# Projecting a tile's heads while its attention still runs: readiness queues, priorities and moved loads in a statically scheduled attention kernel

## The chip, the cores and the metric

The kernel runs on one core of one Trainium2 chip. The metric is the device time of one execution in microseconds (us). Each run's times are compared with runs of the kernel before on the same chip.

## The reference

Two independent attention blocks, A and B, of the same shape are computed and their outputs are put side by side. Cut to what matters:

```python
# per block: x [8, 144, 640], k_cache and v_cache [8, 32, 512, 128], wq [640, 4096], wo [4096, 640], bf16
q = (x @ wq).reshape(8, 144, 32, 128).transpose(0, 2, 1, 3)
scores = einsum("bhqd,bhkd->bhqk", q, k_cache) * 128 ** -0.5
p = softmax(scores)
o = einsum("bhqk,bhkd->bhqd", p, v_cache)
y = o.transpose(0, 2, 1, 3).reshape(8, 144, 4096) @ wo
# result: concatenate([y_A, y_B], axis=-1)
```

## The kernel before

The kernel records operations, each with an engine, an estimated duration and the buffers that it reads and writes. A list scheduler then fixes the order of each engine, in windows of 24 operations, and emits the instructions with the semaphore waits that the buffers ask for. So PE (matmuls), ACT (activations and evictions), DVE (vector work) and the load queue (SP) each run a fixed order, and an operation that waits holds up everything behind it on its engine.

A "tile" is one batch element of one block: 16 tiles, numbered 0 to 15, of four groups of eight heads. In a group PE projects Q (into ps_q, moved to qt_sb by ACT), multiplies with K (ps_s), DVE takes the maximum, ACT the exponential, DVE normalises, PE transposes (ps_pt), DVE copies, PE multiplies with V (ps_o), ACT evicts to otm_sb (the 128 main query rows) and otr_sb (the remaining 16 rows). The output projection takes otm_sb per tile, and otr_sb once per block for all eight batch elements ("the remainder"). Each projection is 32 matmuls of 512 columns and 32 of 128.

```python
# the output projection: "fillers", put between the operations of the NEXT tile's attention
for k in range(H // 4):
    res.append(mk_a(k))          # four heads, 512 columns, PSUM bank ps_out
res.append(ev_a)                 # ACT evicts
for k in range(H // 8):
    res.append(mk_b(k))          # eight heads, 128 columns, same bank
res.append(ev_b)
res.append(dma_out)
...
before(0, lambda: load_wq(0, 0))
before(0, lambda: load_xT(0, 0))
for g in range(1, NG):
    before(g, lambda g=g: load_wq(0, g))
if XH == 2:
    before(1, lambda: load_xT(0, 1))
for hg in range(NHG):
    before(min(2 + hg // 2, NG - 1), lambda hg=hg: load_wo(0, hg))
...
for blk in range(2):
    for b in range(NB):
        fill_state[1] = max(1, FILL_SLOTS // (len(fillers) + 1)) if fillers else 1
        for g in range(NG):
            attention_group(blk, b, g, gi, fillers)   # pops a filler now and then
            ...
        while fillers:
            fillers.pop(0)()
        ...
        fillers.extend(outproj_ops(blk, b))
        if b == NB - 1:
            fillers.extend(outproj_ops(blk, NB))      # the remainder
            ...
while fillers:
    fillers.pop(0)()             # tile 15 and the last remainder stand at the very end
```

Of the kernel before, what the change touches and what calls it, by code (L numbers as in the profile page):

```python
# [22 lines left out]
NPT_BANKS = 2  # L23
SCHED_WINDOW = 24
MODEL_ONLY = False
_DBG = {}


# [23 lines left out]
class _Sched:  # L52
# [3 lines left out]
        self.readers = {}  # L56

    def add(self, eng, fn, reads=(), writes=(), dur=100.0, dma=None, name="", prio=None):
        op = _Op(len(self.ops), eng, fn, tuple(reads), tuple(writes), float(dur), dma, name,
                 len(self.ops) if prio is None else prio)  # L60
        for r in op.reads:
            for w in self.writers.get(r, ()):
                op.preds[w] = "raw"
        for r in op.writes:
            for rd in self.readers.get(r, ()):
                if rd != op.idx and rd not in op.preds:
                    op.preds[rd] = "war"
            for w in self.writers.get(r, ()):
                if w not in op.preds:
                    op.preds[w] = "waw"  # L70
        for r in op.reads:
            self.readers.setdefault(r, []).append(op.idx)
        for r in op.writes:
            if self.readers.get(r) or r not in self.writers:
                self.writers[r] = [op.idx]
            else:
                self.writers[r].append(op.idx)
            self.readers[r] = []
            if r in op.reads:
                self.readers[r] = []  # L80
        self.ops.append(op)
        return op
# [73 lines left out]
def _mm_ns(n):  # L156
    return max(29.0, 2.6 + n * 0.4167)


def _dve_ns(n, mode=1, ptr=0):  # L160
    return 64.0 + n / (0.96 * mode) + 60.0 * ptr


def _act_ns(n, ptr=0, acc=False):
    return 63.0 + n / 1.2 + 88.0 * ptr + (90.0 if acc else 0.0)


def bass_concat_heads__gqa_block_cached__mha_block_cached__near_ridge_kernel(
# [17 lines left out]
    NB, SQ, D = A_x.shape  # L186
    _, H, SK, DH = A_k_cache.shape
# [10 lines left out]
    NG = H // 8  # L198
# [17 lines left out]
    with ExitStack() as st:  # L216
# [62 lines left out]
        def load_wq(blk, hg):  # L279
            wq = blks[blk][3]  # L280
            src = wq.rearrange("(c p) n -> p c n", p=128)[:, :, hg * 1024:(hg + 1) * 1024]
            dst = wq_sb[:, :, hg * 1024:(hg + 1) * 1024]

            def f(e):
                return e.dma_start(dst, src)
            S.add("sp", f, writes=[("wq", hg)], dur=200, dma=(("wq", hg), 128 * NCH * 1024 * 2, "pl"),
                  name="wq%d.%d" % (blk, hg))
# [68 lines left out]
        def softmax_rn(tiles, tag):  # L356
            t0 = tiles[0][0]
            n = len(tiles)
            assert all(tiles[i][0] == t0 + i for i in range(n))

            def f_r(v):
                return v.reciprocal(rr_sb[:, t0:t0 + n], rs_sb[:, t0:t0 + n])  # L362
            S.add("dve", f_r, reads=[("rs", t0 + i) for i in range(n)],
                  writes=[("rr", t0 + i) for i in range(n)], dur=61 + 2 * n, name="R" + tag)
            for i, (ts, pslot) in enumerate(tiles):
                def f_n(v, ts=ts, pslot=pslot):
                    return v.tensor_scalar(p_sb[:, pslot, :], p_sb[:, pslot, :], rr_sb[:, ts:ts + 1], None, ALU.mult)  # L367
                S.add("dve", f_n, reads=[("rr", ts), ("P", pslot)], writes=[("P", pslot)],
                      dur=_dve_ns(512, 4, 1), name="N%s.%d" % (tag, i))

        def attention_group(blk, b, g, gi, fillers):
            gs = gi % NQG
            bs = b % NOB
            slots = load_kv(blk, b, g)
            half = b // BPH
            tg = "%d.%d.%d" % (blk, b, g)

            def fill():
                fill_state[0] += 1
                if fillers and fill_state[0] % fill_state[1] == 0:  # L380
                    fillers.pop(0)()

            for pi in range(4):
                e = 0 if pi < 2 else 1
# [81 lines left out]
            for pi in range(4):  # L466
# [70 lines left out]
                def f_oe(a, pi=pi):  # L537
# [4 lines left out]
                S.add("act", f_oe, reads=[("PSO",)],  # L542
                      writes=[("OTm", bs, g, pi), ("OTr", blk, b, g, pi)],
                      dur=_act_ns(256) + _act_ns(32), name="Oe%s.%d" % (tg, pi))
                fill()

        ost_ctr = [0]

        def outproj_ops(blk, b):
            rem = (b == NB)  # L550
            os_ = ost_ctr[0] % NOS
            ost_ctr[0] += 1
# [4 lines left out]
            def lhs(h):  # L557
                return otr_sb[:, blk, h, :] if rem else otm_sb[:, bs, h, :]
# [7 lines left out]
            def mk_a(k):  # L566
                def go():
                    def f(t):
                        ins = None
                        for h in range(4 * k, 4 * k + 4):  # L570
                            ins = t.matmul(ps_out[:, 0:512], lhs(h), wo_sb[:, h, 0:512],  # L571
                                           start=(h == 0), stop=(h == H - 1))
                        return ins
                    reads = [("wo", (4 * k) // 8)]
                    for h in range(4 * k, 4 * k + 4, 2):
                        reads += rd(h)
                    S.add("pe", f, reads=reads, writes=[("PSOUT",)], dur=4 * _mm_ns(512),
                          name="OPa%s.%d" % (tg, k))
                return go

            def mk_b(k):
                def go():
                    def f(t):
                        ins = None
                        for h in range(8 * k, 8 * k + 8):
                            ins = t.matmul(ps_out[:, 0:D2], lhs(h), wo_sb[:, h, 512:D],  # L586
                                           start=(h == 0), stop=(h == H - 1))
                        return ins
                    reads = [("wo", k)]
                    for h in range(8 * k, 8 * k + 8, 2):  # L590
                        reads += rd(h)
                    S.add("pe", f, reads=reads, writes=[("PSOUT",)], dur=8 * _mm_ns(D2),
                          name="OPb%s.%d" % (tg, k))
                return go

            def ev_a():
                def f(a):
                    return a.copy(ost_sb[:, os_, 0:512], ps_out[:, 0:512])  # L598
                S.add("act", f, reads=[("PSOUT",)], writes=[("ost", os_, 0)], dur=_act_ns(512),
                      name="OEa" + tg)  # L600

            def ev_b():
                def f(a):
                    return a.copy(ost_sb[:, os_, 512:D], ps_out[:, 0:D2])
                S.add("act", f, reads=[("PSOUT",)], writes=[("ost", os_, 1)], dur=_act_ns(D2),
                      name="OEb" + tg)

            def dma_out():
# [12 lines left out]
                              writes=[("out", blk, "r", bb)], dur=200,  # L621
                              dma=(("outr", bb), 16 * D * 2, "pl"), name="OD%s.%d" % (tg, bb))

            for k in range(H // 4):
                res.append(mk_a(k))
            res.append(ev_a)
            for k in range(H // 8):
                res.append(mk_b(k))
            res.append(ev_b)
            res.append(dma_out)  # L630
            return res

        setup_ops()
        FILL_SLOTS = 18 * NG
        fill_state = [0, 1]
        pre = {}

        def before(gi_, fn):
            pre.setdefault(gi_, []).append(fn)

        before(0, lambda: load_wq(0, 0))
        before(0, lambda: load_xT(0, 0))
        for g in range(1, NG):
            before(g, lambda g=g: load_wq(0, g))
        if XH == 2:
            before(1, lambda: load_xT(0, 1))
        for hg in range(NHG):
            before(min(2 + hg // 2, NG - 1), lambda hg=hg: load_wo(0, hg))

        gi = 0  # L650
        fillers = []
        for blk in range(2):
            for b in range(NB):
                fill_state[0] = 0
                fill_state[1] = max(1, FILL_SLOTS // (len(fillers) + 1)) if fillers else 1
                for g in range(NG):
                    for fn in pre.get(gi, ()):
                        fn()
                    attention_group(blk, b, g, gi, fillers)
                    gi += 1  # L660
                    if blk == 0 and b == NB - 1:
                        load_wq(1, g)
                while fillers:
                    fillers.pop(0)()
                if blk == 0 and XH == 2 and b == BPH - 1:
                    load_xT(1, 0)
                if blk == 0 and b == NB - 1:
                    load_xT(1, XH - 1)
                fillers.extend(outproj_ops(blk, b))
                if b == NB - 1:  # L670
                    fillers.extend(outproj_ops(blk, NB))
                    if blk == 0:
                        for hg in range(NHG):
                            fillers.append(lambda hg=hg: load_wo(1, hg))
        while fillers:
            fillers.pop(0)()

        engines = ("pe", "act", "dve", "pool", "sp")
        order = S.schedule(engines, window=SCHED_WINDOW)
# [99 lines left out]
```

## Time and profile before

| | kernel before |
|---|---|
| time, median of the first 5 runs | 809.24 us |
| profiled span | 809.1 us |
| PE, DVE, ACT busy | 92%, 90%, 76% |
| tile 0 ends | 93.0 us |
| a steady tile (4 to 6) | 46.0 us |
| from the last eviction to the end | 19.3 us |

The end of a tile is read from the timeline: 16 small casts to otr_sb belong to each tile, and the end of the 16th is the tile's end. PE's busy time contains the pipeline of its matmuls (a 512-column one lasts 381 ns in the mean, but they follow each other every 216), so 92% is not 92% of what PE can do; the prediction therefore counts matmuls times their spacing. Its fences show the busy shares, the stretches, the load queue and the chain at the end.

### The profile page before, as it was taken

What the parts mean: (1) busy time and instruction counts of PE and PEld (TensorE: products, weight loads), DVE (VectorE), ACT (ScalarE), POOL (GpSimd) and SP (SyncE); (2) the same over time, 40 slices, a digit from 0 to 9 for tenths busy, and PEclk for the clock granted to TensorE, in tenths of its full rate; (3) what the DMA queues carried; (4) which work ended last, traced back from release to release, by engine and by line L of the source; (5) the groups of instructions that cost most, each with busy time, mean ns of one, the idle gap of its engine ahead of it and who ended that gap; (6) DMA issues with size and microseconds to landing.
All of it is one profiled execution on the core that took longest, in us unless ns stands there. A gap on an engine that the chain in (4) does not pass through costs nothing.

```text
span 809.1 us, 23020 instructions
## 1 busy us (share of the span) xinstructions
PE 747.8 (92%) x8946; PEld 569.2 (70%) x9088; DVE 724.6 (90%) x1858; ACT 615.8 (76%) x1957; POOL 0.7 (0%) x6
## 2 busy tenths in 40 slices
PE   3768999999999999999999989999999999999996
PEld 2545687777777777777777667777777778777763
DVE  3665999999999999999998879999999999999990
ACT  2555788888888788888876768788888888888861
POOL 0000000000000000000000000000000000000000
PEclk9789999999999999999999999999999999999999
DMA  9999999989899988799999999997798878888600
GB/s 208 270 275 283 232 247 210 196 182 182 174 227 206 201 182 195 180 213 249 246 218 245 316 234 219 205 194 184 172 201 192 191 179 189 185 187 189 158 5 17
DMA packets 362476, 162.59 MB, mean 201 GB/s; under 512 B 281216, under 2 KB 357248, under 8 KB 362368
## 3 DMA queue, kind: packets, MB, share of 16 engines
q1 hardware_dynamic: 362368, 161.12, 89.6%
q8 instruction: 72, 1.18, 0.7%
q14 instruction: 36, 0.29, 0.1%
HBM read 88.08 MB, written 2.95 MB: 113 GB/s over the span
## 4 chain that ended last, share of the span: by engine, by line
PE 64%; DVE 20%; ACT 8%; DMA 4%; issue 2%; SPq 1%; ACTq 0%
PE ps_q L392 14%; PE ps_o L527 13%; PE ps_out L571 12%; PE ps_pt L500 10%; DVE nm_sb L346 9%; PE ps_s L479 7%; ACT p_sb L350 5%; DVE ptg_sb L516 4%; DVE p_sb L367 4%; PE ps_s L421 4%; PE ps_out L586 2%; ACT otm_sb L540 2%; PE ps_pt L446 2%; DMA kt_sb<-in_B_k_cache_dram 2%; DVE ptg_sb L461 1%
## 5 line engine op out<-in xcount | busy, mean ns | idle before, releaser
L350 ACT ACTIVATE p_sb<-ps_s,nm_sb 128x512 bf16<-128x512 f32 x576 | 396.3, 695 | 49.0 <-DVE nm_sb L346 26.9
L346 DVE TENSOR_REDUCE nm_sb<-ps_s 128x1 f32<-128x512 f32 x576 | 382.3, 680 | 37.7 <-PE ps_s L479 25.2
L392 PE MATMUL ps_q<-xT_sb,wq_sb 128*128 128x144 bf16 x2560 | 207.2, 230 | 16.1 <-DMA xT_sb<-in_A_x_dram 12.3
L392 PEld LDWEIGHTS ps_q<-xT_sb,wq_sb 128*128 128x128 bf16 x2560 | 175.0, 99 | 44.7 <-issue 17.5
L516 DVE COPY ptg_sb<-ps_pt 128x1024 bf16<-128x1024 bf16 x256 | 174.2, 685 | 13.8 <-PE ps_pt L500 12.7
L367 DVE TENSOR_SCALAR p_sb<-p_sb,rr_sb 128x512 bf16<-128x512 bf16 x576 | 181.9, 346 | 2.3
L527 PE MATMUL ps_o<-ptg_sb,v_sb 128*128 128x144 bf16 x2048 | 172.1, 228 | 7.1 <-DVE ptg_sb L516 4.6
L527 PEld LDWEIGHTS ps_o<-ptg_sb,v_sb 128*128 128x128 bf16 x2048 | 136.8, 98 | 43.0 <-DVE ptg_sb L516 21.0
L500 PE MATMUL ps_pt<-id_sb,p_sb 128*128 128x128 bf16 x2048 | 157.0, 221 | 5.5 <-DVE p_sb L367 4.5
L479 PE MATMUL ps_s<-kt_sb,qt_sb 128*128 128x512 bf16 x392 | 145.9, 387 | 15.5 <-ACT p_sb L350 10.6
L540 ACT CAST otm_sb<-ps_o 128x256 bf16<-128x256 f32 x256 | 94.8, 370 | 72.2 <-PE ps_o L527 67.5
L500 PEld LDWEIGHTS ps_pt<-id_sb,p_sb 128*128 128x128 bf16 x2048 | 131.2, 114 | 22.4 <-DVE p_sb L367 14.0
L403 ACT ACTIVATE qt_sb<-ps_q 128x288 bf16<-128x288 f32 x256 | 106.1, 414 | 48.6 <-PE ps_q L392 46.2
L571 PE MATMUL ps_out<-wo_sb,otm_sb 128*128 128x512 bf16 x493 | 128.1, 381 | 3.4 <-DMA wo_sb<-in_B_wo_dram 1.0
L350 ACT ACTIVATION_READ_ACCUMULATOR p_sb<-ps_s,nm_sb 128x1 f32 x576 | 119.6, 208 | 0.0
L571 PEld LDWEIGHTS ps_out<-wo_sb,otm_sb 128*128 128x128 bf16 x512 | 48.7, 98 | 45.6 <-DMA wo_sb<-in_B_wo_dram 1.2
L479 PEld LDWEIGHTS ps_s<-kt_sb,qt_sb 128*128 128x128 bf16 x512 | 48.0, 98 | 43.8 <-ACT p_sb L350 21.1
L362 DVE RECIPROCAL rr_sb<-rs_sb 128x2 f32<-128x2 f32 (+1 forms) x320 | 49.5, 156 | 5.1 <-ACT p_sb L350 4.7
L541 ACT CAST otr_sb<-ps_o 128x32 bf16<-128x32 f32 x256 | 50.0, 195 | 0.0
L421 PE MATMUL ps_s<-kt_sb,qt_sb 128*32 128x512 bf16 x512 | 40.2, 392 | 3.5 <-DMA kt_sb<-in_B_k_cache_dram 2.1
L586 PE MATMUL ps_out<-wo_sb,otm_sb 128*128 128x128 bf16 x512 | 38.6, 219 | 1.7 <-issue 1.0
L586 PEld LDWEIGHTS ps_out<-wo_sb,otm_sb 128*128 128x128 bf16 x512 | 32.2, 98 | 4.2 <-ACT ost_sb L598 1.2
(19 smaller groups left out, 135.2 us busy)
## 6 DMA issues: line engine op xcount, KB each, us to landing
v_sb<-in_A_v_cache_dram SPq DMA_DIRECT2D x64, 512.0 KB, 4.3
v_sb<-in_B_v_cache_dram SPq DMA_DIRECT2D x64, 512.0 KB, 4.3
wq_sb<-in_A_wq_dram SPq DMA_DIRECT2D x4, 1280.0 KB, 7.2
wo_sb<-in_A_wo_dram SPq DMA_DIRECT2D x4, 1280.0 KB, 12.9
wq_sb<-in_B_wq_dram SPq DMA_DIRECT2D x4, 1280.0 KB, 7.5
wo_sb<-in_B_wo_dram SPq DMA_DIRECT2D x4, 1280.0 KB, 8.7
out_dram<-ost_sb SPq DMA_DIRECT2D x16, 160.0 KB, 3.7
kt_sb<-in_A_k_cache_dram SPq DMA_TRANSPOSE x64, 5.8
```

Of the source, the lines that this page charges most:

```text
L346: return v.tensor_reduce(nm_sb[:, ts:ts + 1], ps_s[:, sbank, :], AXL.X, ALU.max, negate=True)
L350: return a.activation(p_sb[:, pslot, :], ps_s[:, sbank, :], ACTF.Exp, bias=nm_sb[:, ts:ts + 1], scale=1.0, accum_out=rs_sb[:, ts:ts + 1])
L367: return v.tensor_scalar(p_sb[:, pslot, :], p_sb[:, pslot, :], rr_sb[:, ts:ts + 1], None, ALU.mult)
L392: ins = t.matmul(ps_q[:, uu * SQ:(uu + 1) * SQ], wq_sb[:, c, h * 128:(h + 1) * 128], xT_sb[:, c, b * SQ:(b + 1) * SQ], start=(c == 0), sto ...
L403: return a.mul(qt_sb[:, gs, 2 * pi:2 * pi + 2, off:off + SQ], ps_q[:, 0:2 * SQ].rearrange("p (u q) -> p u q", u=2), SCALE,)
L479: return t.matmul(ps_s[:, sbank, :], qt_sb[:, gs, u, qoff:qoff + 128], kt_sb[:, slot, (u % 4) * SK:(u % 4 + 1) * SK], start=True, stop=True,)
L500: ins = t.transpose(ps_pt[:, kpt, (uu * 4 + c) * 128:(uu * 4 + c + 1) * 128], pv[:, c, :], id_sb[:],)
L516: return v.tensor_copy(dst, src)
L527: ins = t.matmul(ps_o[:, uu * SQ:(uu + 1) * SQ], v_sb[:, slot, u % 4, c * 128:(c + 1) * 128], ptg_sb[:, gs, u, c, :], start=(c == 0), stop ...
L540: a.copy(otm_sb[:, bs, h0:h0 + 2, :], src[:, :, 0:128])
L571: ins = t.matmul(ps_out[:, 0:512], lhs(h), wo_sb[:, h, 0:512], start=(h == 0), stop=(h == H - 1))
L586: ins = t.matmul(ps_out[:, 0:D2], lhs(h), wo_sb[:, h, 512:D], start=(h == 0), stop=(h == H - 1))
```

## The change

Its intent: do not keep the projection of a tile for the next tile, but put each piece into a queue and let it go once the heads it reads are recorded as done; so that only little stands behind the last tile. Four things change together: the queues with a closer filling stride (a piece may be let go at every second filling point between the attention's operations); a priority table in the scheduler (the projection 150 places later, the Q projection and its eviction 40 earlier) with slightly other duration estimates; the order of the loads; and a second PSUM bank (ps_q, free by then) with its own queue for the last remainder.

```diff
+PRIO = {"OPa": 150, "OPb": 150, "Qp": -40, "Qe": -40}
+FILL_STRIDE = 2
...
-                 len(self.ops) if prio is None else prio)
+                 len(self.ops) + PRIO.get(kind, 0))
...
 def _dve_ns(n, mode=1, ptr=0):
-    return 64.0 + n / (0.96 * mode) + 60.0 * ptr
+    return 65.0 + n / (0.96 * mode) + 64.0 * ptr
...
+                heads_done[(blk, b)] = 8 * g + 2 * pi + 2
...
-            for k in range(H // 4):
-                res.append(mk_a(k))
-            res.append(ev_a)
+            for k in range(H // OPA_HEADS):
+                res.append((OPA_HEADS * (k + 1), (OPA_HEADS * k) // 8, mk_a(k)))
+            res.append((H, None, ev_a))
...
+        before(0, lambda: load_xT(0, 0))
         before(0, lambda: load_wq(0, 0))
-        before(0, lambda: load_xT(0, 0))
...
-            before(1, lambda: load_xT(0, 1))
+            before(BPH * NG - NG, lambda: load_xT(0, 1))
...
-            before(min(2 + hg // 2, NG - 1), lambda hg=hg: load_wo(0, hg))
+            before(NG + hg if NB > 1 else NG - 1, lambda hg=hg: do_load_wo(0, hg))
...
+        def eligible(item):
+            blk, b, nh, hg, fn, tsn = item
+            if hg is not None and (blk, hg) not in wo_loaded:
+                return False
+            if b == NB:
+                return all(heads_done.get((blk, bb), 0) >= nh for bb in range(NB))
+            return heads_done.get((blk, b), 0) >= nh
...
+                tile_ops = outproj_ops(blk, b)
+                queues[0].extend(tile_ops)
...
+                    if last and g == NG - 1:
+                        queues[1].extend(outproj_ops(blk, NB, acc=ps_q, acc_res=("PSQ",)))
```

## The prediction

> **What bounds the kernel now.** I read the page's busy shares first, then the windows view cut at tile ends, then the timeline of start and end. A "tile" is one batch element of one block: four groups of eight heads, 16 tiles in all. Its end is the 16th small cast at L541 that belongs to it, counted in the timeline. Those ends are 92.9, 136.4, 181.9, 227.5, 273.7, 319.3, 365.5, 411.1, 465.6, 515.7, 561.2, 606.8, 653.1, 698.8, 744.9 and 789.7 us; so most tiles take 45.4 to 46.2 us, and four stretches stand out: tile 0 (92.9), tile 8 (54.5), tile 9 (50.1) and 19.4 us after the last tile.
>
> ```profile
> PE 747.8 (92%) x8946; PEld 569.2 (70%) x9088; DVE 724.6 (90%) x1858; ACT 615.8 (76%) x1957; POOL 0.7 (0%) x6
> ...
> DMA  9999999989899988799999999997798878888600
> ```
>
> ```profile
> 12.00:93.00 81.00, 62.73 (x612) 43.52 (x618) 52.19 (x130) 45.78 (x138) 0.00 (x0) 0.87 1.09 266
> ...
> 182.00:228.00 46.00, 44.97 (x558) 34.93 (x565) 45.02 (x116) 38.37 (x123) 0.00 (x0) 1.00 0.93 182
> ...
> 411.00:466.00 55.00, 52.58 (x611) 39.12 (x618) 45.32 (x115) 39.86 (x127) 0.00 (x0) 1.00 1.07 258
> 466.00:516.00 50.00, 47.26 (x581) 37.04 (x592) 45.98 (x122) 38.13 (x124) 0.00 (x0) 0.97 1.04 224
> ...
> 790.00:809.00 19.00, 11.61 (x99) 6.82 (x98) 0.00 (x0) 1.70 (x4) 0.00 (x0) 0.93 0.06 18
> ```
>
> Columns: stretch, length, busy us of PE, PEld, DVE, ACT, POOL, then clock, DMA share, GB/s. In an ordinary tile (182 to 228) PE and DVE are both busy 98%: nothing idle is left to fill. In tile 0 DVE works 52 of 81 us while DMA moves 266 GB/s against 182 later: the start is **bound by loads**. In 411 to 466, where tile 7 and the remainder rows of block A are both projected, DVE has slack: that tile is **bound by PE**. After 790 only PE works.
>
> Why the start is slow stands in the timeline of the load queue:
>
> ```profile
> 28.99 4.07 SPq L326 DMA_TRANSPOSE kt_sb<-in_A_k_cache_dram  x1
> 33.10 0.58 SPq L331 DMA_DIRECT2D v_sb<-in_A_v_cache_dram  x1
> 33.73 0.52 SPq L285 DMA_DIRECT2D wq_sb<-in_A_wq_dram  x1
> 34.28 2.93 SPq L295 DMA_DIRECT2D wo_sb<-in_A_wo_dram  x2
> 37.33 12.43 SPq L326 DMA_TRANSPOSE kt_sb<-in_A_k_cache_dram  x1
> ```
>
> The K transpose behind three weight loads occupies the queue 12.43 us instead of about 3.9. From 33.73 to 49.76 the queue handled three weight loads and one K: 16.0 less 3.9 is 12.1 us, **4.0 us per weight load**. The next group repeats it (55.02 to 70.85: 11.9 us for three).
>
> The tail is the last part of the chain of work that ended last:
>
> ```profile
> 789.79 1.05 PE ps_out L571 x4
> ...
> 791.51 1.98 PE ps_out L586 x32
> ...
> 794.05 6.87 PE ps_out L571 x31
> ...
> 801.59 1.98 PE ps_out L586 x32
> ```
>
> These are the last four wide matmuls of tile 15, its 32 narrow ones, then all 64 of the remainder, serialised by evictions in one bank (ps_out). From PE's end at 803.56 to 809.1 there are 5.5 us of eviction and store.
>
> **What the Trainium skill says.** "TensorE: Matmul & The Clock Gate", section Back-to-back issue gap, puts the isolated warm gap at N/2.4 + 2.5 ns: 215.8 for 512 columns, 62.5 for 144, 55.8 for 128. The trace agrees: 31 matmuls of 512 in 6.85 us, last one 0.38 long, is 216 ns; 32 of 128 in 1.96 us is 56 ns. I use these gaps, not the rows' means (381 and 219 ns), which contain the pipeline. "Perfetto Trace Analysis", section Optimization Strategy, says that where the most-contended engine changes over time, interleaving those regimes may help. That is the intent here: tail and start are the other regimes. "DMA: Bandwidth & Descriptors", section Issuing engines are not separate DMA queues, says all DMAs run on the same 16 engines; the 12.43 us issue agrees that weights and K share one capacity. So moving weights later relieves tile 0 but charges tile 1.
>
> **The change, part by part.** Counts are of the built program: matmuls on PE between tile ends, times the gaps above (a packed 32-column matmul at a quarter of 216). No arithmetic is added: 711.9 us of PE work before, 711.5 after, DVE work the same. How time relates to that work is read from before: tiles with 42.8, 43.0, 43.8 us of PE work took 45.4, 45.6, 46.2, and the double tile with 52.3 took 54.5. So a tile takes its **PE work plus about 2.3 us**, if loads arrive and DVE's 45 us allow.
>
> *Loads.* wo moves from groups 2 and 3 to groups 4 to 7, one per group; the second half of x moves to group 12. Tile 0 then has one weight load per group. Going on from the first V pair issued at 17.2, each group costs 4.0 for wq and 2 x 4.5 for its K and V, 13.0 in all: the last K of tile 0 leaves the queue at 55.6 instead of 75.4, about 20 us sooner. But tile 1 now has the wo loads, again 13.0 per group against some 11.4 of compute: its last K leaves at 55.6 + 52 = 107.6, against 112.5 before. Before, tile 0 ended 17.5 us after its last K, 4.3 us of it out-projection that is now gone; I take 15 for tile 1: **122.6 instead of 136.4**, 14 us gained. (xT now precedes wq at the very start; I give that 0 to 1.5 us.)
>
> *Backlog.* Tile 0 has no wo, so its projection moves on: the order puts 0 us of projection in tile 0, 6.8 in tile 1, 14.8 in tile 2, 9.5 in tile 3 (before: 4.3, 7.9, 8.5, 8.7). Tiles 2 and 3 hold 46.8 and 46.9 us of PE work, so about 49 each against 45.4 and 45.6: **7 us given back**. Tiles 4 to 7 hold 43.1, 43.4, 43.3, 45.0, a sum of 174.8 plus 9.2, or 184.0 against 183.6 measured: nothing.
>
> *Block change.* Tile 7's projection is nearly complete when tile 7 ends, so tile 8 holds 45.6 us of PE work instead of 52.3: 47.9. Tile 9 gets 47.4 instead of 44.0. The four wo loads of block B still go out together behind the remainder's projection; before, tile 9 took 50.1 where its 44.0 plus 2.3 gives 46.3, so I charge some 3 us for them again: 52.7. Together 100.6 against 104.6: **4 us gained**.
>
> *Steady tiles 10 to 14.* Work shifts by tenths; 0. Tile 15 holds 42.9 against 41.4: 1 us lost.
>
> *Tail.* After the last value product the order has 12 wide and 64 narrow matmuls: 12 x 0.216 + 64 x 0.056 = 6.2 us, with ps_q as a second bank hiding the evictions. Plus 0.3 and the 5.5 us of last eviction and store: 12.0. Before it was 19.4: **7.4 us gained**.
>
> Sum: -14 + 7 + 0.4 - 4 + 1 - 7.4 = -17. 809.2 - 17 = 792; finer placing of projections and earlier Q projections (priority -40) may take a little from the waits, so I put 791.
>
> **Rivals.**
> 1. *PE is not the bound in steady tiles, DVE is* (724.6 us less 4.6 of memsets, over 16 tiles, is 45.0 of some 45.7). Then the backlog in tiles 2 and 3 fits partly into slack, and only some 3 us return: about 785. For it: DVE's 98%. Against: the 2.3 us rule also fits the double tile, in which DVE had slack.
> 2. *The load bill is only postponed.* Bytes up to tile 1's end fall only by half of x, so the load gain could shrink to the 5 us by which the last K leaves sooner: about 800. For it: DMA share 1.09. Against: before, by the end of tile 1, K ran nearly two groups ahead, a lead which the change can spend.
> 3. *The fixed order hits new waits*: held ps_out accumulations, or Q projections placed ahead of weights not yet landed, which block PE in order. Some 5 to 10 us in the start or at the block change: 797 to 801. For it: the chain before shows a 7.80 us wait for wq in tile 0; against: wq now comes sooner.
>
> **Range and chances.** 2% faster is 793.1, near my sum; loads are the uncertain term (5 to 18 us), then the steady tiles (12 of them, each 0.5 us either way: 6 us). So 780 to 802, and 0.57 for faster, 0.41 for the same, 0.02 for slower, which would take two of the rivals at their worst.
>
> **What would show it.** Tile 0 should end near 71, tile 1 near 123, tiles 2 and 3 take about 49 each, tiles 4 to 7 184 together, tiles 8 and 9 about 101 together, and the end come 12 us after the last cast. The weight loads should no longer stretch a K issue past about 8 us in the first 60 us. If tile 1 ends after 128, rival 2 holds; if tiles 2 and 3 take 46, rival 1; if steady tiles change by over 0.5 us, the priorities do more than I allow, and my sum is wrong there.

## The result

The changed kernel takes **792.42 us** in the median of 9 runs (790.32 to 796.33) against 809.24 us (15 runs, 806.55 to 813.28). The ratio is 0.9795, with a 95% interval of 0.9773 to 0.9816. So it is about 2% faster; whether by more or less than 2% is not decided by the interval. Ratios here and below are the mean time of one kernel's fast runs over that of the other's of the same rounds, so not quite the ratio of the medians.

The page of the changed kernel, in the lines that answer to those shown of before:

```profile
PE 737.7 (93%) x8939; PEld 567.1 (72%) x9088; DVE 719.9 (91%) x1858; ACT 613.9 (78%) x1957; POOL 0.7 (0%) x6
...
DMA  7999999999998978899999999988888888889720
```

PE's busy time fell by 10 us although it does the same work. The clock was low for a shorter part of the start (0.87 of full speed over 81 us before, 0.92 over 66 us now); whether that is all of the 10 us is not shown. The stretches of the changed kernel, with the same columns as in the prediction, cut at its own tile ends:

```profile
11.00:77.00 66.00, 53.77 (x600) 40.08 (x609) 51.11 (x127) 44.76 (x139) 0.00 (x0) 0.92 1.11 272
...
268.00:312.00 44.00, 43.43 (x544) 33.85 (x549) 43.19 (x115) 36.60 (x117) 0.00 (x0) 1.00 0.81 188
...
357.00:411.00 54.00, 48.38 (x584) 37.87 (x590) 46.37 (x120) 39.92 (x129) 0.00 (x0) 0.97 1.06 244
411.00:458.00 47.00, 45.30 (x557) 34.91 (x567) 43.50 (x115) 36.71 (x119) 0.00 (x0) 1.00 1.00 236
...
779.00:790.00 11.00, 5.41 (x73) 4.22 (x71) 0.00 (x0) 1.71 (x4) 0.00 (x0) 0.86 0.10 30
```

Tile 0 now takes until 77 us instead of 93, an ordinary tile 44 to 45 us instead of 46, and the end 11 us instead of 19. But the stretch from 357 to 411, which is tile 7, takes 54 us with PE busy for 48: something new waits there.

All tile times, read as above, in us (one profiled execution each; single entries of the start and of tile 7 differ by 1 to 2 us between executions of the same instruction order, as the entries of the runs that share it show):

| kernel | tile 0 ends | tile 1 | tiles 2+3 | mean of 4 to 6 | tile 7 | tiles 8+9 | mean of 10 to 14 | tile 15 | end | span |
|---|---|---|---|---|---|---|---|---|---|---|
| before | 93.0 | 43.5 | 91.1 | 46.0 | 45.6 | 104.6 | 45.8 | 44.7 | 19.3 | 809.1 |
| changed | 76.7 | 50.5 | 96.3 | 44.6 | 53.4 | 98.2 | 45.2 | 43.9 | 11.2 | 789.9 |
| e1 no priorities | 75.8 | 50.7 | 99.6 | 48.0 | 48.0 | 110.6 | 48.2 | 49.3 | 11.1 | 830.0 |
| e2 before + priorities | 93.4 | 44.0 | 89.1 | 45.2 | 52.0 | 100.8 | 45.0 | 43.8 | 20.3 | 804.1 |
| e3 old loads | 92.7 | 43.9 | 89.7 | 44.8 | 54.2 | 98.0 | 45.2 | 43.9 | 11.2 | 793.9 |
| e4 one bank | 75.7 | 50.6 | 96.3 | 44.6 | 51.7 | 98.0 | 45.2 | 44.1 | 19.3 | 795.4 |
| e5 projection priority only | 77.7 | 48.2 | 99.5 | 45.7 | 45.8 | 103.0 | 46.3 | 45.7 | 12.0 | 800.7 |
| e6 Q priority only | 75.3 | 50.5 | 96.6 | 46.5 | 52.9 | 106.0 | 46.5 | 47.4 | 11.1 | 811.8 |
| e7 late x | 74.8 | 49.7 | 96.3 | 44.6 | 45.1 | 102.1 | 45.3 | 44.3 | 11.2 | 783.7 |
| e8 late x, gated wo | 76.5 | 49.5 | 96.3 | 44.6 | 47.3 | 105.3 | 46.3 | 43.9 | 11.2 | 795.3 |
| e9 old durations | 76.1 | 51.5 | 96.6 | 44.6 | 53.0 | 104.4 | 44.7 | 43.9 | 12.9 | 796.0 |
| e10 stride 4 | 75.5 | 50.5 | 91.4 | 45.4 | 54.5 | 89.9 | 46.9 | 45.5 | 15.5 | 793.3 |
| e11 late x, tile 8 later | 76.2 | 50.4 | 96.3 | 44.6 | 45.1 | 102.5 | 45.3 | 44.2 | 11.2 | 785.9 |

The load queue of the changed kernel at the end of tile 0's loads:

```profile
43.22 0.51 SPq L294 DMA_DIRECT2D wq_sb<-in_A_wq_dram  x1
43.83 7.50 SPq L335 DMA_TRANSPOSE kt_sb<-in_A_k_cache_dram  x1
51.37 0.58 SPq L340 DMA_DIRECT2D v_sb<-in_A_v_cache_dram  x1
52.05 4.17 SPq L335 DMA_TRANSPOSE kt_sb<-in_A_k_cache_dram  x1
```

A K transpose behind one weight load holds the queue 7.50 us, not 12.43 as behind three, and the last K of tile 0 leaves it at 56.2 us (52.05 + 4.17).

The chain that ended last, at its end:

```profile
779.11 0.86 PE ps_out L578 x4
779.97 0.86 PE ps_q L578 x4
780.83 0.89 PE ps_out L593 x16
781.73 0.45 PE ps_q L593 x8
782.17 0.45 PE ps_out L593 x8
```

The two projections alternate between ps_out and ps_q, and no eviction stands between them. Of the 6.9 us and twice 2 us of matmuls in one bank that the prediction shows, only these short pieces are left behind the last tile.

Tile 7's wait, in the order of PE:

```profile
395.28 0.79 PE L396 MATMUL ps_q<-xT_sb,wq_sb 128*128 128x144 bf16 x10
400.89 0.73 PE L425 MATMUL ps_s<-kt_sb,qt_sb 128*32 128x512 bf16 x8 [4.82 <-DMA kt_sb<-in_B_k_cache_dram]
401.55 1.14 PE L531 MATMUL ps_o<-ptg_sb,v_sb 128*128 128x144 bf16 x8
402.91 1.41 PE L396 MATMUL ps_q<-xT_sb,wq_sb 128*128 128x144 bf16 x10 [0.22 <-issue]
```

PE stands 4.82 us for the first K of block B. Then ten Q matmuls take 1.41 us instead of 0.79: the trace shows the clock at half for the 3.41 us from 401.25 us on (the last section compares this with the Trainium skill). And the load queue at that time:

```profile
382.15 0.45 SPq L294 DMA_DIRECT2D wq_sb<-in_B_wq_dram  x1
382.65 9.55 SPq L315 DMA_TRANSPOSE xT_sb<-in_B_x_dram  x5
392.30 6.22 SPq L335 DMA_TRANSPOSE kt_sb<-in_B_k_cache_dram  x2
```

The K is issued only at 392.30, behind five transposes of x. They load the second half of block B's x, which no tile before tile 12 reads.

### The profile page after: what moved, and what is told of

It is laid out like the page before. It is cut to its first block, busy times and chain, and to the rows that moved or that the text cites. A ratio compares the mean times of both kernels' runs of the same rounds, so it can differ in the third digit from the quotient of the medians.

```text
span 789.9 us, 22973 instructions
## 1 busy us (share of the span) xinstructions
PE 737.7 (93%) x8939; PEld 567.1 (72%) x9088; DVE 719.9 (91%) x1858; ACT 613.9 (78%) x1957; POOL 0.7 (0%) x6
## 4 chain that ended last, share of the span: by engine, by line
PE 76%; ACT 8%; DVE 7%; DMA 6%; issue 1%; SPq 1%; ACTq 0%
PE ps_q L396 18%; PE ps_o L531 14%; PE ps_out L578 13%; PE ps_pt L504 11%; PE ps_s L483 9%; PE ps_s L425 4%; ACT p_sb L359 4%; PE ps_out L593 4%; DVE nm_sb L355 3%; DMA kt_sb<-in_A_k_cache_dram 2%; DMA kt_sb<-in_B_k_cache_dram 2%; DVE ptg_sb L520 2%; ACT otm_sb L544 2%; PE ps_pt L450 2%; DVE p_sb L376 1%
## 5 line engine op out<-in xcount | busy, mean ns | idle before, releaser
L531 PEld LDWEIGHTS ps_o<-ptg_sb,v_sb 128*128 128x128 bf16 x2048 | 139.1, 98 | 35.4 <-DVE ptg_sb L520 10.6
L407 ACT ACTIVATE qt_sb<-ps_q 128x288 bf16<-128x288 f32 x256 | 107.0, 418 | 53.7 <-PE ps_q L396 50.6
L483 PE MATMUL ps_s<-kt_sb,qt_sb 128*128 128x512 bf16 x380 | 138.3, 384 | 8.2 <-ACT p_sb L359 4.3
L544 ACT CAST otm_sb<-ps_o 128x256 bf16<-128x256 f32 x256 | 95.1, 371 | 45.5 <-PE ps_o L531 41.6
L578 PEld LDWEIGHTS ps_out<-wo_sb,otm_sb 128*128 128x128 bf16 x512 | 48.5, 98 | 44.8 <-issue 1.3
L483 PEld LDWEIGHTS ps_s<-kt_sb,qt_sb 128*128 128x128 bf16 x512 | 47.7, 98 | 25.6 <-ACT p_sb L359 10.8
L545 ACT CAST otr_sb<-ps_o 128x32 bf16<-128x32 f32 x256 | 50.4, 197 | 0.0
```

What stands on the lines that cost most here:

```text
L407: return a.mul(qt_sb[:, gs, 2 * pi:2 * pi + 2, off:off + SQ], ps_q[:, 0:2 * SQ].rearrange("p (u q) -> p u q", u=2), SCALE,)
L483: return t.matmul(ps_s[:, sbank, :], qt_sb[:, gs, u, qoff:qoff + 128], kt_sb[:, slot, (u % 4) * SK:(u % 4 + 1) * SK], start=True, stop=True,)
L531: ins = t.matmul(ps_o[:, uu * SQ:(uu + 1) * SQ], v_sb[:, slot, u % 4, c * 128:(c + 1) * 128], ptg_sb[:, gs, u, c, :], start=(c == 0), stop ...
L544: a.copy(otm_sb[:, bs, h0:h0 + 2, :], src[:, :, 0:128])
L578: ins = t.matmul(acc[:, 0:512], lhs(h), wo_sb[:, h, 0:512], start=(h == 0), stop=(h == H - 1))
```

## The experiments

Eleven kernels ran, with three rounds each. All gave correct results.

**e1: no priorities.**

```diff
-PRIO = {"OPa": 150, "OPb": 150, "Qp": -40, "Qe": -40}
+PRIO = {}
```

> The changed kernel with an empty priority table, nothing else altered. Theory P (the priorities, above all the Q projections moved 40 places ahead, take the waits out of the steady tiles: 44.4 to 44.7 us in tiles 4 to 6 of the changed kernel against 45.6 to 46.2 before): tiles 4 to 6 go back to about 45.7, and the wait of 4.8 us on K in tile 7 shrinks, since the weights of block B are then freed and loaded later; total 792 to 798. Rival D (the finer placing of the out-projection does it, not the priorities): tiles 4 to 6 stay at about 44.6, total 786 to 792.

Measured: 827.11 us, ratio 1.0236 to the kernel before (1.0201 to 1.0271). Both theories had the total too low: without its priorities the interleaving is slower than the kernel before. A steady tile takes 48.0 us. The waits between 200 and 350 us, in this kernel (line: who waited for whom, total us, times, longest; PEld is PE's weight load):

```profile
PEld ps_s L483 <- ACT p_sb L359: 10.8, 24, 0.8
...
PEld ps_out L578 <- ACT otr_sb L545: 4.1, 9, 0.7
```

and in the changed kernel, where no wait of ps_out on ACT is listed in that stretch:

```profile
PEld ps_s L483 <- ACT p_sb L359: 1.1, 3, 0.4
```

The second line of e1 is the projection standing right behind the eviction that it needs; the first is PE waiting for ACT to read a score bank so that it can be written again. Theory P holds for the direction: the priorities take waits out of the steady tiles. The wait on K in tile 7 did vanish, as it expected (48.0 us, like its neighbours).

**e2: the kernel before with the priorities alone.** The same table and the lookup by name were put into the kernel before.

```diff
+PRIO = {"OPa": 150, "OPb": 150, "Qp": -40, "Qe": -40}
...
-                 len(self.ops) if prio is None else prio)
+                 len(self.ops) + PRIO.get(kind, 0))
```

> The kernel before with the priority table of the change alone. Theory P: tiles 4 to 6 fall from 45.6 to 46.2 us to about 44.7, so some 10 us in all over 12 steady tiles, less a possible new wait on K at the block change: 797 to 803. Rival D: the steady tiles stay at 45.7 and the total at 806 to 811. The end after the last cast stays near 19 us in both, since the remainder is still projected last and in one bank.

Measured: 805.45 us, ratio 0.9958 (0.994 to 0.9976). Tiles 4 to 6 take 45.2 us on average, 0.8 less than before, and 10 to 14 take 45.0; but tile 7 takes 52.0 instead of 45.6. So the priorities save about 0.8 us per steady tile here, and the new wait at the block change eats most of it. Counted as in the prediction, the matmuls between this trace's ends of tiles 3 and 6 are 43.8 us of PE work per tile, so the overhead is 1.4 us, where three tiles of the kernel before have 2.4 to 2.6 in the prediction's figures: nearly the 1.3 of the whole change. The total lies between the two expectations: P was right in kind and too large in size.

**e3: the changed kernel with the old order of loads.**

```diff
-        before(0, lambda: load_xT(0, 0))
         before(0, lambda: load_wq(0, 0))
+        before(0, lambda: load_xT(0, 0))
...
-            before(BPH * NG - NG, lambda: load_xT(0, 1))
+            before(1, lambda: load_xT(0, 1))
...
-            before(NG + hg if NB > 1 else NG - 1, lambda hg=hg: do_load_wo(0, hg))
+            before(min(2 + hg // 2, NG - 1), lambda hg=hg: do_load_wo(0, hg))
```

> The changed kernel with the order of loads of the kernel before (first wq before x, wo in groups 2 and 3, second half of x in group 1). Theory of the prediction, with the measured sizes (tile 1 ends 9.3 us sooner thanks to the loads, tiles 2 and 3 give 5.3 back): tile 0 ends near 93, tile 1 near 136, but tiles 2 and 3 take only some 44.6 each instead of 48.0 and 48.3, so the total rises by 2 to 4 us only: 794 to 797. Rival (the loads are the main gain, the backlog would have come anyway): +8 to +10, 800 to 803.

Measured: 795.54 us, ratio 0.9831 (0.9808 to 0.9853), 3.1 us above the changed kernel's median. Tile 0 ends at 92.7 us and tile 1 takes 43.9, as expected; tiles 2 and 3 together take 89.7 instead of 96.3. So the moved loads bring tile 1's end from 136.6 forward to 127.2 us (9.4 us), and the backlog gives 6.6 us of it back. The net size is uncertain: the interval of this run (0.9808 to 0.9853) just touches that of the changed kernel (0.9773 to 0.9816), and the two were measured in different batches. The rival, 800 to 803, lies outside it and falls. Between e2 and this run the span falls by 10.2 us, 9.1 of them at the end (20.3 to 11.2): in sum, what the queues add to the priorities is the short end.

**e4: the last remainder in the common queue and bank.**

```diff
-                    if last and g == NG - 1:
-                        queues[1].extend(outproj_ops(blk, NB, acc=ps_q, acc_res=("PSQ",)))
...
         heads_done[(1, -1)] = 0
+        queues[0].extend(outproj_ops(1, NB))
```

> The changed kernel with the last remainder projection put behind tile 15 in the common queue and bank, as before, instead of a queue and a bank of its own. Theory of the prediction (the last tile takes 24 wide matmuls of the remainder for about 1 us, and the second bank hides the evictions): the end after the last cast grows from 11.2 to about 18 or 19 us, tile 15 gets at most 1 to 2 us shorter, total +6 to +7: 798 to 799.5. Rival (the PE is full, so moved work only changes place): tile 15 gets 5 us shorter, total +2 to +3, the part that the evictions take.

Measured: 798.85 us, ratio 0.9879 (0.985 to 0.9908), 6.4 us above the changed kernel's median. The end takes 19.3 us again and tile 15 takes 44.1 instead of 43.9. The 24 wide matmuls of the remainder that the change puts into tile 15 cost nothing visible there. Without them the tile holds only 36.4 us of PE work (counted in this trace) and still takes 44.1: here the rule of PE work plus 2.3 us does not hold. DVE is the busier engine in that stretch (40.83 of 44 us; PE's 39.62 contain the pipeline), but no run here shows that it is the bound:

```profile
732.00:776.00 44.00, 39.62 (x457) 28.16 (x454) 40.83 (x105) 32.64 (x107) 0.00 (x0) 1.00 0.44 88
```

The rival (PE is full, moved work only changes place) falls for the last tile. No Q projection of a following tile is left to do there.

**e5: only the projection's priority.** The table is {"OPa": 150, "OPb": 150}.

> The changed kernel with only the out-projection's priority (150 places later), Q projections at their own place. Theory R, after the run without any priorities: right behind the eviction that it reads, an out-projection makes PE wait for ACT (4.1 us in 9 waits between 200 and 350 us); the 150 places of distance remove that, and the Q projections matter little: steady tiles 4 to 6 at 44.5 to 45.2 us, total 792 to 799. Rival Q (the early Q projections take the waits away): tiles 4 to 6 near 48, total above 815.

Measured: 800.79 us, ratio 0.9908 (0.9884 to 0.9932). Tiles 4 to 6 take 45.7 us: better than 48.0, short of 44.6, and the total misses the expected range by 2 us. Waits on ACT between 200 and 350 us:

```profile
PEld ps_s L483 <- ACT p_sb L359: 5.1, 14, 0.6
```

No wait of the projection on ACT is listed there any more, while half of the wait for score banks remains.

**e6: only the Q projections' priority.** The table is {"Qp": -40, "Qe": -40}.

> The changed kernel with only the Q projections' priority (40 places earlier), the out-projection at its own place. Theory R: tiles 4 to 6 stay near 48 us, total 818 to 828. Rival Q: tiles 4 to 6 at about 45, total 790 to 800.

Measured: 813.92 us, ratio 1.0077 (1.0023 to 1.0132). Tiles 4 to 6 take 46.5 us. Here the two waits are the other way round:

```profile
PEld ps_out L578 <- ACT otr_sb L545: 6.4, 16, 0.7
...
PEld ps_s L483 <- ACT p_sb L359: 1.9, 4, 0.6
```

So neither theory R nor rival Q is right alone. Each entry removes its own wait: the late projection removes the one on the eviction, the early Q projection most of the one on the score banks. From 48.0 us per tile the first alone saves 2.3, the second alone 1.5, both together 3.4. The listed waits are of PE's weight loads and are not all on the path, so they do not add up to these savings; how the rest of the 3.4 us divides stays open.

**e7: the second half of block B's x later.**

```diff
+                if blk == 1 and XH == 2 and b == 1:
+                    load_xT(1, 1)
                 if blk == 0 and XH == 2 and b == BPH - 1:
                     load_xT(1, 0)
                 if blk == 0 and b == NB - 1:
-                    load_xT(1, XH - 1)
```

> The changed kernel with the second half of block B's x, which is needed from tile 12 on, loaded after tile 9 instead of after tile 7. Theory X: its five transposes and the wq load with them (9.55 us of queue time from 382.65 us) stand ahead of the first K of block B and make the 4.8 us wait in tile 7; without them tile 7 falls from 53.4 to 45.5 to 47 us and the total by 5 to 7 us, to 785 to 788. Rival: the four wq loads of block B keep K late by themselves, the wait shrinks by half at most: 789 to 791.

Measured: **786.04 us**, ratio 0.9727 (0.9695 to 0.9759). Theory X holds: the first K of block B is issued right behind the wq load, at 379.68 us instead of 392.30, tile 7 takes 45.1 us, and in its stretch PE is busy for nearly all of it at full clock.

```profile
379.14 0.45 SPq L294 DMA_DIRECT2D wq_sb<-in_B_wq_dram  x1
379.68 10.90 SPq L335 DMA_TRANSPOSE kt_sb<-in_B_k_cache_dram  x2
```

```profile
355.00:400.00 45.00, 44.37 (x553) 34.70 (x561) 43.96 (x115) 38.30 (x124) 0.00 (x0) 1.00 1.14 258
400.00:453.00 53.00, 49.74 (x587) 37.44 (x595) 46.04 (x119) 38.38 (x123) 0.00 (x0) 0.97 1.02 244
```

This version beats both kernels: its interval lies below that of the changed kernel (0.9773 to 0.9816). Of the 8.3 us won in tile 7, 3.9 come back in tiles 8 and 9 (102.1 instead of 98.2): tile 8 now has a wait for block B's first wo load.

```profile
PE ps_out L578 <- DMA wo_sb<-in_B_wo_dram: 2.6, 1, 2.6
```

**e8: in addition the four wo loads of block B let go one by one.** The load items are taken out of the queue and recorded from the filling points, each made to wait for a fresh eviction (x goes after tile 10 here):

```diff
-                    for hg in range(NHG):
-                        queues[0].append((1, -1, 0, None, lambda hg=hg: do_load_wo(1, hg), NB - 1))
+                    late_wo.extend(range(NHG))
...
+            since[0] += 1
+            rem_left = any(it[0] == 0 for it in queues[0])
+            if late_wo and not rem_left and since[0] >= WO_GAP:    # 26 filling points
+                do_load_wo(1, late_wo.pop(0), gate=[last_oe[0]])   # gate: a buffer that the load "reads"
+                since[0] = 0
```

> As the run before (x after tile 10 here), and in addition the four wo loads of block B let go one by one, each behind an eviction some 26 filling points after the one before, instead of all together. If the bunch of four loads is what costs tile 9 its 3 us above PE work plus 2: total 2 to 4 us below the run before, 782 to 786. If tile 9 is simply full of PE work (47.4 us): no change against the run before, since the same projections only move to tile 10.

Measured: 796.39 us, ratio 0.9846 (0.982 to 0.9871), 10 us slower than e7. Neither expectation holds. The gates made wo late, and PE waits for it three times in tile 9 (until 463.56, 485.26 and 503.13 us), which takes 56.3 us:

```profile
PE ps_out L579 <- DMA wo_sb<-in_B_wo_dram: 8.2, 3, 4.7
```

So the bunch is better than gates of this spacing; other spacings were not tried.

**e9: the old duration estimates.** The changed kernel with 64/60 for DVE, 88/90 for ACT and 61 for the reciprocal in its scheduler.

```diff
-    return 65.0 + n / (0.96 * mode) + 64.0 * ptr
+    return 64.0 + n / (0.96 * mode) + 60.0 * ptr
```

> The changed kernel with the duration estimates of the kernel before in its static scheduler (64 and 60 instead of 65 and 64 for DVE, 88 and 90 instead of 90 and 92 for ACT, 61 instead of 68 for the reciprocal). If they matter only by chance of order: steady tiles 4 to 6 within 0.5 us of 44.6, total 788 to 797. If they carry the gain of the steady tiles: tiles 4 to 6 near 45.7, total 800 or more.

Measured: 792.92 us, ratio 0.9814 (0.9769 to 0.986); tiles 4 to 6 take 44.6 us. Its interval contains the changed kernel's ratio. The new estimates carry none of the gain in the steady tiles, and the total differs by no more than the noise. (The profiled execution in the table is the slowest of this run's four, 797.75 us.)

**e10: a filler at every fourth filling point.**

```diff
-FILL_STRIDE = 2
+FILL_STRIDE = 4
```

> The changed kernel with a filler at every fourth instead of every second filling point, which is about the spacing of the kernel before; the order of PE then leaves 9.6 us of projection behind the last value product instead of 6.2. If the closer spacing matters only for readiness at the end: the end after the last cast grows from 11.2 to about 14.5 us, the steady tiles stay at 44.6, tiles 2 and 3 (43.7 and 44.5 us of PE work instead of 46.8) get 2 us shorter each and pass their work to tiles 10 and 15, total 791 to 797. If close placing makes the steady tiles: tiles 4 to 6 near 45.7, total 800 or more.

Measured: 795.35 us, ratio 0.9834 (0.9804 to 0.9865). The end takes 15.5 us. Tiles 2 and 3 take 91.4 instead of 96.3 us, tiles 8 and 9 89.9 instead of 98.2: work only moves on, and it comes back mostly in tile 10 (51.4 instead of 45.1). Tiles 4 to 6 take 45.4, 0.8 more than 44.6, where the first expectation had no change. Most of that is work too: the matmuls between the tile ends are 43.9 us of PE work per tile in this trace against 43.2 in e4's, which has the changed kernel's tile times there. That the spacing itself matters in steady tiles is not shown.

**e11: e7, with the projection of tile 8 a further 60 places later.**

```diff
-                 len(self.ops) + PRIO.get(kind, 0))
+                 len(self.ops) + PRIO.get(kind, 0) + (60 if name.startswith(("OPa1.0.", "OPb1.0.")) else 0))
```

> The run with the late x of block B, and in addition the projection of tile 8 a further 60 places later, so that its first four matmuls stand 14 rows further down PE's order. If the wait on the first wo load of block B (2.6 us, with the clock low after it) is what is left in tile 8 (53.0 us for 46.9 us of PE work): tile 8 falls by 3 to 4 us, total 782 to 784. If K or the bunch of wo loads hold tile 8 anyway: 785 to 788.

Measured: 787.04 us, ratio 0.9739 (0.9697 to 0.978), the same as e7 within the intervals. Tile 8 fell from 53.0 to 48.8 us as hoped, and tile 9 rose from 49.1 to 53.7. The wait was not the bound of the two tiles together: they take 102.5 us against 102.1. PE now waits 2.44 us in tile 9 for a K of block B, and the clock is at half for the 3.41 us from 465.13 us on, as it was after the wo wait in e7:

```profile
464.21 0.62 PE L425 MATMUL ps_s<-kt_sb,qt_sb 128*32 128x512 bf16 x8 [2.44 <-DMA kt_sb<-in_B_k_cache_dram]
```

So one wait went and another came. What holds the pair was not settled; both tiles hold over 46 us of PE work, and four wo loads fall into them.

## Why the prediction was right

The number (791 against 792.42) came out right, and the mechanism held at its start and end. That it came so close is luck: the first two tiles gained 4.7 us less than reckoned and tile 7 cost 7.8 us that the sum did not hold, while the steady tiles gave 7.5 us that it had as nothing and tiles 8 and 9 another 2.4. Point by point, with the differences of the two profiled spans:

- **Loads (-14 predicted).** The queue was reckoned well: last K of tile 0 out at 55.6 us, measured 56.2; last K of tile 1 at 107.6, measured 110.2. Tile 1 ended at 127.2 us, not 122.6, a gain of 9.3 us: the term was too large by 4.7. Tile 1 ended 17.0 us after its last K left the queue, where the prediction chose 15; and tile 0 ended at 76.7 us, 20.5 after its last K, where the prediction expected 71. The x-before-wq order let PE's first matmul start at 13.63 us instead of 12.35. Over all runs it starts at 13.60 to 14.28 us with the new order and at 10.52 to 12.35 with the old (before, e2, e3), so the order costs some 2 us, where 0 to 1.5 was given.
- **Backlog (+7).** Tiles 2 and 3 took 48.0 and 48.3 us, 5.2 more than before. e3 shows that it belongs to the moved loads: with the old order it is gone. Rival 2 (the bill is only postponed, total 800) was half of the truth: the moved loads are worth some 3 us net, where the two terms gave 7.
- **Tiles 4 to 7 (+0.4) and 10 to 14 (0).** This is the step that failed in kind. The prediction said that steady time is PE work plus 2.3 us, whatever the order. Tiles 4 to 6 lost 4.3 us in all and 10 to 14 lost 3.2, with nearly the same work. e1, e2, e5 and e6 show that the overhead depends on the order: without priorities it is 4.6 us (48.0 us for 43.4 us of work), with both 1.3 (the prediction's own three ordinary tiles give 2.4 to 2.6, a little above its 2.3), and the waits that go with the priorities in e1, e5 and e6 are those on ACT for evicted heads and for score banks. The 2.3 us of the kernel before are made up differently. Between 200 and 350 us it has no wait of the projection for evicted heads, its waits for score banks are 3.4 us in 9, and its longest wait on an engine is the value product's for DVE's copy:

```profile
PEld ps_o L527 <- DVE ptg_sb L516: 4.9, 18, 0.4
```

This is 0.8 us in 4 waits in the changed kernel. No run takes that wait out alone, so how much of the gain over the kernel before is owed to it stays open. The prediction had named this sign itself ("if steady tiles change by over 0.5 us, the priorities do more than I allow").

- **Tile 7, not foreseen.** It rose by 7.8 us to 53.4, through a wait for the first K of block B behind an x load that was not yet needed. Rival 3 named the kind (a fixed order that hits new waits, at the block change), but the sum had nothing for it. e7 shows the cause by removing it. e2 shows that the priorities bring it on: with them alone, the kernel before has it too (52.0 us), while e1 without them has not. Of the two entries it is that of the Q projections: e6, with this one alone, has the wait (3.65 us, tile 7 at 52.9), and e5, with the other alone, has not (45.8).
- **Tiles 8 and 9 (-4).** They took 6.4 us less, for the reason given (tile 7's projection was already out of the way), and 2.4 more than reckoned.
- **Tile 15 (+1).** It got 0.8 us shorter; e4 shows that the remainder's matmuls there were free, so this term, too, failed by the rule of PE work plus 2.3 us. (Its own difference, 42.9 less 41.4, is 1.5 and was entered as 1.)
- **Tail (-7.4).** Measured -8.1; e4 gives 6.4 us of the median back when the second queue and bank are taken away.

The measured terms sum to -9.3 + 5.2 - 4.3 + 7.8 - 6.4 - 3.2 - 0.8 - 8.1 = -19.1, which is the difference of the two spans before they are rounded. Taken part by part in one order, from medians: the priorities 809.1 to 805.45 (e2), the queues with the new tail to 795.54 (e3), the loads to 792.42. The order matters: without the priorities the same queues cost time (e1).

Rival 1 (DVE is the bound of steady tiles) fell where it was staked: tiles 2 and 3, with some 46.8 us of PE work each, did not fit into any slack. For the tiles 4 to 6 it is not ruled out. In the changed kernel DVE is busy there for 131.8 of 134 us, or 98%, as it was before; that leaves it no more room than PE, which has 43.3 us of work in 44.6. In tile 15, e4 speaks for something other than PE. No run made DVE's work smaller, so which of the two bounds a steady tile now stays open.

## What to carry to other kernels

Interleaving dependent work into an in-order engine paid here only with distance between producer and consumer: the same queues made the kernel 2.4% slower than before without a priority table and 2% faster with it. When a load is moved or an engine runs ahead, look through the load queue for transfers that are not needed yet and stand before those that are; moving one x load gave another 5 to 6 us. An overhead per tile that is the same in all tiles is not a constant of the machine: ask which waits it is made of before carrying it into the prediction.

## What the Trainium skill lacked or had wrong

- "TensorE: Matmul & The Clock Gate", section Back-to-back issue gap, gives about 81 ns at 128 columns and 131 ns at 512 for a stream of weight loads and matmuls in a real kernel, and calls its formula for single matmuls an over-count at 512. Here, with a weight load for each matmul, the rows of the tail give 56 ns and 216 ns: the single-matmul formula holds and the stream figures do not.
- "DMA: Bandwidth & Descriptors", section Issuing engines are not separate DMA queues, calls the sequencer's time to start a DMA usually small beside the DMA. The plain loads agree (wq 0.5 us, of 7.2 us in the median from issue to landing), but a K transpose holds the issuing queue for about 3.9 us, of 5.8 us to landing, and 12.43 us behind three weight loads.
- No page that we read tells how far a consumer on PE should stand behind its producer on ACT in a fixed order. Here, between 200 and 350 us, PE's weight loads waited 14.9 us on ACT for score banks and evicted heads (10.8 + 4.1) without the priorities and 1.1 us with them.
- "TensorE: Matmul & The Clock Gate", section Why this matters for your kernels, warns of PE gaps above some 3 us, after which the clock is back at half. Tile 7's wait of 4.82 us agrees with it, but shorter ones are enough: the clock was also at half for 3.41 us after PE waited 2.62 us (e7), 2.44 (e11), 2.39 (e6) and 2.13 (before). It stayed full after 2.28 us (e3), 2.36 (e10) and 2.13 (e8).
